# Denominator without the GpSimd pass, four chunk pairs to a logarithm visit, two diagonal convolutions, a new order

## The chip, the cores and the metric

One NeuronCore of a Trainium2 chip. Its engines run their own instruction streams in order and wait for each other by semaphores: TensorE (PE in the views, PEld for its weight loads), VectorE (DVE), ScalarE (ACT), GpSimd (POOL), and SyncE (SP), which here only issues DMAs. The metric is the device time of one execution in microseconds (us), lower is better.

## The reference

A causal convolution over time with softmax weights per head, then two feed-forward layers for 8192 tokens of 192 channels.

```python
w = softmax(weight, axis=-1)                       # 8 heads, 7 taps
x = sum_k w[head, k] * x_padded[:, s + k, :]       # (2, 4096, 192)
x = x.reshape(8192, 192)
gate = 1 / (1 + exp(-(x @ w_gate)))                # 192 -> 1536
x = (gate * (x @ w_val)) @ w_out                   # 1536 -> 192
h = x @ w_in                                       # 192 -> 2048
P = a[0] + a[1]*h + a[2]*h**2 + a[3]*h**3
Q = 1 + abs(b[0])*abs(h) + abs(b[1])*h**2
out = (P / (Q + 1e-6)) @ w_out2                    # 2048 -> 192
```

The matrices of both layers come as float64, two 32-bit words each, and the kernel turns them into float32 on the chip; x and the result are float32.

## The kernel before

The tokens stand along the free axis, in 16 tiles of 512. Each tile goes through three stages. `conv` makes the convolution of channels 0 to 127 (`ca`) and of 128 to 191 (`cb`, for two tiles at once). `moe1` is the gated layer in 12 chunks of 128 hidden channels, and `moe2` the rational layer in 16 chunks, which are taken in 8 pairs of 1024 columns. To keep float32 precision each matrix operand is split into a high part rounded to fp32r and the rest (`xha` and `xla`, `xhb` and `xlb`, `yha` and so on), so that a chunk of a 192-row product takes five matmuls (`mm192`, L656 to L660), and a chunk of an output product also five (L663 to L669). A tile takes 24 x 5 + 12 x 5 + 16 x 5 + 16 x 5 = 340.

`moe1`: the gate's and the value's sums land in PSUM banks `w` (four). ScalarE takes the sigmoid, VectorE multiplies by the value (L704), and the product is split into `r` tiles. At the end the sums `accb` are taken out of PSUM (L725 and its neighbours) and split into the y tiles, which `moe2` reads.

`moe2`, for one pair: ScalarE reads h from PSUM twice, as u = a3*h + a2 (two pointer operands, tile `av`) and as |h| (no pointer). VectorE makes the rest of P (L773, L775). GpSimd makes n = b1*|h| + b0 (L778), VectorE n*max(|h|, 1e-9) (L783). The quotient goes by a logarithm and a sigmoid, 1/(1 + q) = sigmoid(-ln q): ScalarE takes Ln and then Sigmoid of the pair, VectorE multiplies (L796), and the result is split: the high part by ScalarE, VectorE or GpSimd (L376, L375, L372), the rest by VectorE (L387). Ln and Sigmoid stand in different tables of ScalarE, so a change between them puts in an ACT_TABLE_LOAD. A visit to the logarithm takes two pairs (`batch`), so that a tile of 8 pairs makes four visits. `f` tiles (12 of 128x1024) hold s, u, |h| and n; `r` tiles (7) the split products.

The first tile's convolution differs: for channels 0 to 127 PE multiplies by seven diagonal matrices, made by VectorE from an identity (`conv_first`), and for the others VectorE runs the seven taps (L572, L575). Later tiles are convolved by GpSimd (L580, L583).

The order of all engines' instructions is decided when the program is built, by `Plan.order`: a list scheduler with costs of its own in ns, which takes the operation with the lowest priority number that can start. `PRM` holds offsets to the priorities (`off`), how many tiles each use may hold (`caps`), and what it costs in priority to hand a copy to another engine (`alt`). One line of the clock model reads

```python
step = 0.4473 if self.cols.get(w - 1, 0.0) >= BUSY else 0.8386
```

Of the kernel before, what the change touches and what calls it, by code (L numbers as in the profile page):

```python
# [75 lines left out]
class Plan:  # L76
# [72 lines left out]
    def order(self, look, switch):  # L149
# [78 lines left out]
        "g.m": 12836, "g.l": -14036, "gv": -503688, "gv.f": 39931, "gv.s": 21424, "gv.m": -105715,
        "ha": 14068, "ha.f": -9127, "ha.m": -20059, "ha.l": -563873, "hi1": -461921, "hi1.f": 117595,
        "hi1.m": 30632, "hi1.l": 9352, "hi2": 617179, "hi2.s": 28015, "hi2.l": -67281, "ld": 85904,  # L230
        "ld.m": 66018, "ln": -94912, "ln.f": 56900, "ln.s": 26766, "ln.m": -50067, "lo1": -192199,
        "lo1.f": -196745, "lo1.m": -47345, "lo1.l": 151726, "lo2": -186968, "lo2.f": -41762, "lo2.m": -14603,
# [5 lines left out]
        "wA.m": -6466, "wA.l": -16824, "wB": -78045, "wB.f": 31019, "wB.s": 8326, "wB.m": 53803, "wB.l": 1311,
        "wC": -20347, "wC.s": 22921, "wC.m": 34154, "wC.l": 40145, "wD": -203, "wD.f": 5940, "wD.s": -20677,
        "wD.m": -48332, "wD.l": 27289, "xs": -1058521, "xs.f": 114386, "xs.s": 6043, "xs.m": -67359,  # L240
        "xs.l": -82500, "y": -644733, "y.f": 64816, "y.s": -60589, "y.m": -7966, "ye": 91, "ye.f": -70525,
        "ye.s": -105007, "ye.m": 10681, "ye.l": 132694, "late": 6944, "ld.f": -71783, "lo2.s": -107566,
# [640 lines left out]
```

## Time and profile before

| | |
|---|---|
| median of 3 runs | 1328.44 us (1327.5 to 1329.65) |
| profiled execution, own time | 1329.45 us |
| its span | 1327.7 us |
| PE busy | 1279.2 us |
| VectorE busy | 1208.6 us |
| ScalarE busy | 1182.8 us |
| GpSimd busy | 654.0 us |

The span is the time from the program's first to its last instruction in the profile; the execution's own time holds a little more around it. A busy time is a union of instructions' times. PE's matmuls overlap in the records, so PE's own is no measure of how near it is to its best.

### The profile page before, as it was taken

The numbers are of one execution on the slowest core, as the hardware profiler recorded it, in microseconds if no ns is written. First come the engines' busy times: TensorE is split into PE (matmuls) and PEld (weight loads), VectorE is DVE, ScalarE is ACT, GpSimd is POOL, SyncE is SP. The second block draws the span as 40 slices with busy tenths as digits, with TensorE's granted clock in tenths as the row PEclk, the third lists the DMA queues.
The fourth block names the chain that finished last, engine by engine and source line by source line (L and its number), as shares of the span: only waits on it lengthen the run. The fifth ranks groups of instructions, "written<-read, shape, count | busy, mean of one in ns | idle before, by whom it ended". The sixth has DMA issues, their size and how long they took to land.

```text
span 1327.7 us, 15365 instructions
## 1 busy us (share of the span) xinstructions
PE 1279.2 (96%) x5478; PEld 1020.7 (77%) x5478; DVE 1208.6 (91%) x1410; ACT 1182.8 (89%) x1556; POOL 654.0 (49%) x450
## 2 busy tenths in 40 slices
PE   8889999999999999999999999999999999999996
PEld 4677778778777777788788877878787787877775
DVE  7889999999899989999888989899989998989897
ACT  6988989889998998889889988988989989999996
POOL 4166627735275542865429572394725836212131
PEclk9989999999999999999999999999999999999999
DMA  6621000000000000000000000000000000000000
GB/s 173 198 61 32 8 1 13 16 13 9 0 13 17 13 8 1 12 17 13 9 9 5 16 21 1 12 1 17 20 1 13 8 13 1 0 13 13 1 6 19
DMA packets 14317, 27.09 MB, mean 20 GB/s; under 512 B 2080, under 2 KB 5792, under 8 KB 14240
## 3 DMA queue, kind: packets, MB, share of 16 engines
q1 hardware_dynamic: 14240, 26.11, 6.7%
q8 instruction: 43, 0.70, 0.2%
q14 instruction: 34, 0.28, 0.1%
HBM read 19.81 MB, written 6.29 MB: 20 GB/s over the span
## 4 chain that ended last, share of the span: by engine, by line
PE 42%; DVE 26%; ACT 23%; issue 6%; DMA 2%; POOL 1%; SPq 0%; ACTq 0%; DVEq 0%; POOLq 0%
ACT f L376 14%; DVE r L387 6%; PE w L656 5%; PE w L657 5%; PE w L658 5%; PE w L660 5%; PE w L659 5%; DVE f L773 5%; ACT L376 4%; DVE f L775 4%; DVE f L783 4%; DVE f L796 3%; ACT r L376 2%; PE accd L668 2%; PE accd L669 2%
## 5 line engine op out<-in xcount | busy, mean ns | idle before, releaser
L778 POOL TENSOR_SCALAR f<-f,bv 128x1024 f32<-128x1024 f32 x128 | 189.2, 1479 | 435.2 <-ACT f L376 371.5
L376 ACT ACTIVATE f<-w 128x512 f32<-128x512 f32 x448 | 260.6, 599 | 48.9 <-PE w L660 25.4
L387 DVE TENSOR_TENSOR r<-f,r 128x1024 fp32r<-128x1024 f32 x224 | 292.1, 1316 | 10.6 <-ACT r L376 7.1
L376 ACT ACTIVATE f<-f 128x1024 f32<-128x1024 f32 (+3 forms) x288 | 286.6, 1002 | 1.5 <-DVE r L387 0.3
L376 ACT ACTIVATE f<-w,av 128x512 f32<-128x512 f32 x256 | 196.9, 778 | 43.8 <-PE w L660 39.1
L376 ACT ACT_TABLE_LOAD x160 | 205.3, 1283 | 2.9 <-DVE f L783 0.2
L376 ACT ACTIVATE r<-f 128x1024 fp32r<-128x1024 f32 x180 | 189.7, 1062 | 19.5 <-DVE f L704 9.8
L773 DVE TENSOR_TENSOR f<-f,w 128x512 f32<-128x512 f32 x256 | 170.5, 679 | 33.8 <-ACT f L376 32.9
L775 DVE SCALAR_TENSOR_TENSOR f<-f,av,w 128x512 f32<-128x512 f32 x256 | 187.0, 740 | 6.4 <-ACT f L376 3.3
L796 DVE SCALAR_TENSOR_TENSOR f<-f,av,f 128x1024 f32<-128x1024 f32 x128 | 175.1, 1380 | 12.8 <-ACT f L376 12.7
L783 DVE SCALAR_TENSOR_TENSOR f<-f,f 128x1024 f32<-128x1024 f32 x128 | 173.2, 1355 | 0.8 <-POOL f L778 0.6
L704 DVE TENSOR_TENSOR f<-f,w 128x512 f32<-128x512 f32 x192 | 130.3, 679 | 34.4 <-ACT f L376 23.0
L583 POOL TENSOR_TENSOR ca<-ca,tmp 128x512 f32<-128x512 f32 x90 | 154.2, 1713 | 6.0
L580 POOL TENSOR_SCALAR tmp<-xa,cw 128x512 f32<-128x512 f32 x90 | 115.4, 1282 | 8.4 <-DMA xa<-in_xt 1.4
L656 PE MATMUL w<-yha,w_h 128*128 128x512 f32 x256 | 102.1, 399 | 4.9 <-DVE f L775 3.2
L663 PE MATMUL accd<-r,wo_s 128*128 128x512 f32 x256 | 100.9, 394 | 4.9 <-ACT r L376 2.6
L668 PE MATMUL accd<-r,wo_s 128*128 128x512 f32 x256 | 100.8, 394 | 4.4 <-DVE r L387 4.3
L665 PE MATMUL accd<-r,wo_s 128*128 128x512 f32 x256 | 100.2, 391 | 0.3 <-DVE f L820 0.2
L669 PE MATMUL accd<-r,wo_s 128*128 128x512 f32 x256 | 100.2, 391 | 0.0
L664 PE MATMUL accd<-r,wo_s 128*128 128x512 f32 x256 | 100.0, 391 | 0.0
L657 PE MATMUL w<-yha,w_l 128*128 128x512 f32 x256 | 99.8, 390 | 0.0
L659 PE MATMUL w<-yhb,w_b 128*128 128x512 f32 x256 | 99.8, 390 | 0.0
(104 smaller groups left out, 2859.8 us busy)
## 6 DMA issues: line engine op xcount, KB each, us to landing
f<-in_wo SPq DMA_DIRECT2D x14, 384.0 KB, 3.3
xa<-in_xt SPq DMA_DIRECT2D x16, 259.0 KB, 2.8
out_dram<-f SPq DMA_DIRECT2D x16, 256.0 KB, 2.0
xb<-in_xt SPq DMA_DIRECT2D x16, 129.5 KB, 2.7
f<-in_w SPq DMA_DIRECT2D x4, 512.0 KB, 4.2
out_dram<-f SPq DMA_DIRECT2D x16, 128.0 KB, 2.3
f<-in_wg SPq DMA_DIRECT2D x4, 256.0 KB, 4.2
f<-in_wv SPq DMA_DIRECT2D x4, 256.0 KB, 4.8
```

Source lines behind the costliest of these rows:

```text
L376: plan.op("ACT", (53 if psum else 95) + n * 0.832 + 93 * ptr, prio, lambda: nc.scalar.activation(out=out(), in_=in_(), func=func, **kw), r ...
L387: dve(prio, n, lambda: nc.vector.tensor_tensor(out=out(), in0=in0(), in1=f(in1()), op=ALU.subtract), rd, wr, lock=lock, alts=alts)
L583: plan.op("POOL", 322 + 2.105 * n, p, lambda d=d: nc.gpsimd.tensor_tensor(out=y(), in0=y(), in1=T(d)[0:np_, 0:n], op=ALU.add), rd=[d, acc] ...
L656: nc.tensor.matmul(o, lhsT=wh.tile[:, c], rhs=ha, start=True, stop=False)
L657: nc.tensor.matmul(o, lhsT=wl.tile[:, c], rhs=ha, start=False, stop=False)
L659: nc.tensor.matmul(o, lhsT=wb.tile[:, c], rhs=hb, start=False, stop=False)
L704: dve(at("gv", t, p), n, lambda sc=sc, val=val: nc.vector.tensor_tensor(out=sc(), in0=sc(), in1=val(), op=ALU.mult), [(pv, "v"), (s, i)], ...
L773: dve(at("v", t, p), sn, lambda q=q, cut=cut, h=h: nc.vector.tensor_tensor(out=cut(u[q]), in0=cut(u[q]), in1=h(), op=ALU.mult), [ps_, (u[q ...
L775: dve(at("w", t, p), sn, lambda q=q, cut=cut, h=h: nc.vector.scalar_tensor_tensor(out=cut(u[q]), in0=cut(u[q]), scalar=av.tile[:, 1:2], in ...
L778: plan.op("POOL", 328 + 0.832 * gn, at("n", t, p), lambda q=q: nc.gpsimd.tensor_scalar(C(n[q]), C(ha[q]), bv.tile[:, 1:2], bv.tile[:, 0:1] ...
L783: dve(at("y", t, p), gn, lambda q=q: nc.vector.scalar_tensor_tensor(out=C(n[q]), in0=C(ha[q]), scalar=1e-9, in1=C(n[q]), op0=ALU.max, op1= ...
L796: dve(at("g", t, p), gn, lambda k=k: nc.vector.scalar_tensor_tensor(out=C(u[k]), in0=C(u[k]), scalar=av.tile[:, 0:1], in1=C(n[k]), op0=ALU ...
```

## The change

It does four things. The GpSimd pass over |h| goes: ScalarE's Abs scales by b1 while it reads (a pointer into a new tile `kv`), VectorE's one instruction makes (|b1 h| + b0)*|b1 h|, and the logarithm divides by b1 and adds a tiny constant through its own scale and bias (two pointers into `kv`). No `n` tile is used. A visit to the logarithm takes four pairs (`batch=[4, 4]`; the last tile keeps its four visits of two). The first tile's second convolution, like the first, becomes seven products with diagonal matrices on PE, and ScalarE copies its sum from PSUM to `cb`. And the offsets, caps and hand-over costs are new numbers, so that all engines' orders are new; in the clock model a column costs 0.4427 instead of 0.4473.

```diff
-            step = 0.4473 if self.cols.get(w - 1, 0.0) >= BUSY else 0.8386
+            step = 0.4427 if self.cols.get(w - 1, 0.0) >= BUSY else 0.8386
...
-        "A": -640, "A.f": 5683, "A.s": 4966, "A.m": 12771, "A.l": 26485, "B": 15953, "B.f": 8482,
+        "A": -2963, "A.f": -9114, "A.s": 6869, "A.m": 8851, "A.l": 10628, "B": 16339, "B.s": 720310,
...
-    caps=dict(u=7, n=8, ha=10, s=6, h1=3, l1=2, h2=2, l2=2, raw=3, t=9, dg=5),
+    caps=dict(u=12, ha=20, s=29, h1=13, l1=5, h2=2, l2=27, raw=8, t=3, dg=9),
...
-    batch=[2, 2, 2, 2],
+    batch=[4, 4],
...
-        dve(START + 90001, 1, lambda: nc.vector.tensor_scalar(
-            bv.tile[:, 0:1], bv.tile[:, 0:1], 1e-9, 0.0, op0=ALU.max, op1=ALU.add), [bv], [bv])
+
+        def ks():
+            k = kv.tile
+            nc.vector.tensor_scalar(k[:, 0:1], bv.tile[:, 1:2], 1e-15, 0.0, op0=ALU.max, op1=ALU.add)
+            nc.vector.reciprocal(k[:, 1:2], k[:, 0:1])
+            nc.vector.tensor_scalar(k[:, 1:2], k[:, 1:2], 1.0 / ONE, 0.0, op0=ALU.mult, op1=ALU.add)
+            nc.vector.memset(k[:, 2:3], 1e-18)
+        plan.op("DVE", 650, START + 90001, ks, rd=[bv], wr=[kv])
...
-            conv_taps("cb", t, p0 + step * 7, step, xb, 1, cb, len(two) * R, n, eng)
+            if t:
+                conv_taps("cb", t, p0 + step * 7, step, xb, 1, cb, len(two) * R, n)
+            else:
+                dma(START + 1, 128 * 512, lambda: nc.sync.dma_start(out=T(eye)[:, 0:128], in_=ident), [eye])
+                ca = conv_first(n, xa, 0, eye)
+                cp = conv_first(n, xb, 1, eye)
+                act(START + 19, n, lambda: T(cb)[:, 0:n], lambda: T(cp)[:, 0:n], [cp], [cb], psum=True)
...
-                act(at("ha", t, p), sn, lambda q=q, cut=cut: cut(ha[q]), h, [ps_], [(ha[q], j)], psum=True,
-                    func=ACTF.Abs)
+                act(at("ha", t, p), sn, lambda q=q, cut=cut: cut(ha[q]), h, [ps_, kv], [(ha[q], j)], psum=True,
+                    func=ACTF.Abs, scale=kv.tile[:, 0:1])
...
-            plan.op("POOL", 328 + 0.832 * gn, at("n", t, p), lambda q=q: nc.gpsimd.tensor_scalar(
-                C(n[q]), C(ha[q]), bv.tile[:, 1:2], bv.tile[:, 0:1], op0=ALU.mult, op1=ALU.add),
-                rd=[ha[q], bv], wr=[n[q]], lock=True, alts=[("DVE", 190 + 0.522 * gn, lambda q=q: nc.vector.tensor_scalar(
-                    C(n[q]), C(ha[q]), bv.tile[:, 1:2], bv.tile[:, 0:1], op0=ALU.mult, op1=ALU.add),
-                    True, H["n"]["DVE"])])
+
             dve(at("y", t, p), gn, lambda q=q: nc.vector.scalar_tensor_tensor(
-                out=C(n[q]), in0=C(ha[q]), scalar=1e-9, in1=C(n[q]), op0=ALU.max, op1=ALU.mult),
-                [ha[q], n[q]], [n[q]])
+                out=C(ha[q]), in0=C(ha[q]), scalar=bv.tile[:, 0:1], in1=C(ha[q]), op0=ALU.add, op1=ALU.mult),
+                [ha[q], bv], [ha[q]], ptr=1)
...
-                act(at("ln", t, p + 0.1 * i), gn, lambda k=k: C(n[k]), lambda k=k: C(n[k]), [n[j] for j in qs], [n[k]],
-                    func=ACTF.Ln, table="ln", scale=1.0 / ONE)
+                act(at("ln", t, p + 0.1 * i), gn, lambda k=k: C(ha[k]), lambda k=k: C(ha[k]),
+                    [*(ha[j] for j in qs), kv], [ha[k]], func=ACTF.Ln, table="ln", scale=kv.tile[:, 1:2], bias=kv.tile[:, 2:3])
```

The first place is ScalarE in the middle of the program, one whole visit to the logarithm before (an f tile out of the same f tile at 128x1024 is a logarithm, or a sigmoid behind the second load; `w,av` is u, `w` alone at f is |h| or a moe1 sigmoid):

```order
L376 ACT_TABLE_LOAD
L376 ACTIVATE f_4190<-f_4190 128x1024
L376 ACTIVATE f_4252<-w_4227,av 128x512
L376 ACTIVATE f_4211<-f_4211 128x1024
L376 ACTIVATE f_4252<-w_4239,av 128x512
L376 ACTIVATE f_4271<-w_4227 128x512
L376 ACTIVATE f_4271<-w_4239 128x512
L376 ACT_TABLE_LOAD
L376 ACTIVATE f_4217<-w_4254 128x512
```

and a visit now (`kv` marks the logarithm at 128x1024 and |b1 h| at 128x512):

```order
L378 ACT_TABLE_LOAD
L378 ACTIVATE f_4064<-f_4064,kv 128x1024
L378 ACTIVATE r_4281<-f_4209 128x1024
L378 ACTIVATE f_4140<-f_4140,kv 128x1024
L378 ACTIVATE f_4292<-w_4272,av 128x512
L378 ACTIVATE f_4160<-f_4160,kv 128x1024
L378 ACTIVATE f_4309<-w_4272,kv 128x512
L378 ACTIVATE f_4203<-f_4203,kv 128x1024
L378 ACTIVATE f_4292<-w_4302,av 128x512
L378 ACTIVATE f_4309<-w_4302,kv 128x512
L378 ACT_TABLE_LOAD
L378 ACTIVATE f_4335<-w_4286 128x512
```

Four logarithms stand between two loads instead of two, with PSUM reads that need no table between them in both.

The second place is VectorE at the start, where the low parts of tile 0's convolved input (`xlb`, `xla`) are made among the splits of the weights (`wg`, `wv`; `f` to `f` rows put their words together), before:

```order
L470 SCALAR_TENSOR_TENSOR f_169<-f_169,f_136 128x256
L470 SCALAR_TENSOR_TENSOR f_179<-f_179,f_140 128x256
L387 TENSOR_TENSOR xlb_192<-cb_138,xhb_187 64x512 x2
L387 TENSOR_TENSOR wv_l<-f_169,wv_h 128x256
L387 TENSOR_TENSOR wg_l<-f_179,wg_h 128x256
L470 SCALAR_TENSOR_TENSOR f_183<-f_183,f_146 128x256
L387 TENSOR_TENSOR xla_211<-w_151,xha_203 128x512
```

and now:

```order
L479 SCALAR_TENSOR_TENSOR f_239<-f_239,f_191 128x512
L479 SCALAR_TENSOR_TENSOR f_242<-f_242,f_203 128x512
L479 SCALAR_TENSOR_TENSOR f_247<-f_247,f_218 128x512
L389 TENSOR_TENSOR wv_l<-f_239,wv_h 128x512
L473 TENSOR_SCALAR f_237<-f_237 128x384
L389 TENSOR_TENSOR wg_l<-f_242,wg_h 128x512
L473 TENSOR_SCALAR f_245<-f_245 128x384
L389 TENSOR_TENSOR xlb_269<-cb_257,xhb_263 64x512 x2
L389 TENSOR_TENSOR wg_b<-f_247,wg_b 64x512
```

`xlb` was made between the first and the second column piece of the weights, and now stands among the fourth and last.

The third place is VectorE near the end, from the add that takes the last tile's moe1 sums out of PSUM (L725, now L733), before:

```order
L725 TENSOR_TENSOR f_10498<-f_10498,accb_10240 128x512
L387 TENSOR_TENSOR yla_10514<-accb_10239,yha_10507 128x512
L387 TENSOR_TENSOR r_10521<-f_10092,r_10509 128x1024
L387 TENSOR_TENSOR ylb_10530<-f_10498,yhb_10516 128x512
L387 TENSOR_TENSOR r_10534<-f_10175,r_10523 128x1024
L773 TENSOR_TENSOR f_10550<-f_10550,w_10536 128x512
L775 SCALAR_TENSOR_TENSOR f_10550<-f_10550,av,w_10536 128x512
```

and now:

```order
L733 TENSOR_TENSOR f_10244<-f_10244,accb_9822 128x512
L389 TENSOR_TENSOR r_10272<-f_9926,r_10262 128x1024
L389 TENSOR_TENSOR yla_10282<-accb_9821,yha_10270 128x512
L389 TENSOR_TENSOR ylb_10286<-f_10244,yhb_10276 128x512
L798 SCALAR_TENSOR_TENSOR f_9998<-f_9998,av,f_10030 128x1024
L798 SCALAR_TENSOR_TENSOR f_10074<-f_10074,av,f_10124 128x1024
L779 TENSOR_TENSOR f_10305<-f_10305,w_10291 128x512
```

Products of the tile before (L798, formerly L796) now stand behind the add: from here to the end there are 12 of them, where there were 8.

## Rows read from the trace of the kernel before

**Rows 1.** The page, busy time (share of the span) and instructions of each engine.

```profile
PE 1279.2 (96%) x5478; PEld 1020.7 (77%) x5478; DVE 1208.6 (91%) x1410; ACT 1182.8 (89%) x1556; POOL 654.0 (49%) x450
```

**Rows 2.** Timeline of PE: start, duration, line, tiles; first and last of fifteen.

```profile
23.64 0.39 PE L656 MATMUL w<-xha,wv_h 128*128 128x512 f32 x1
...
26.82 0.39 PE L660 MATMUL w<-xlb,wv_b 128*128 128x512 f32 x1
```

**Rows 3.** Table by stage: length; PE, PEld, DVE, ACT, POOL busy; clock, DMA share, GB/s.

```profile
0.00:154.70 154.70, 139.67 (x562) 105.07 (x563) 133.38 (x194) 129.43 (x217) 80.25 (x64) 0.97 0.34 100
154.70:1260.30 1105.60, 1085.07 (x4696) 873.85 (x4695) 1016.52 (x1151) 999.93 (x1273) 557.78 (x375) 1.00 0.03 10
1260.30:1327.70 67.40, 54.42 (x223) 41.80 (x222) 58.74 (x67) 53.46 (x68) 15.96 (x12) 0.97 0.04 12
0.00:20.00 20.00, 15.26 (x43) 6.66 (x44) 14.18 (x32) 12.02 (x30) 2.18 (x7) 0.98 0.68 188
40.00:60.00 20.00, 18.74 (x82) 14.88 (x81) 18.32 (x35) 17.57 (x33) 0.00 (x0) 1.00 0.80 229
```

**Rows 4.** Chain of work that ended last, 154.7 to 1260.3 us, shares by line.

```profile
by line: ACT f L376 15.1%; DVE r L387 5.9%; issue 5.5%; PE w L656 5.4%; ACT L376 5.0%; PE w L658 5.0%; PE w L660 4.9%; PE w L657 4.9%; PE w L659 4.9%; DVE f L773 4.4%; DVE f L775 3.9%; DVE f L783 3.4%; DVE f L796 3.3%; ACT r L376 2.7%; PE a
```

**Rows 5.** Waits, 154.7 to 1260.3 us: us in total, times, longest.

```profile
DVE f L773 <- ACT f L376: 28.2, 43, 1.8
DVE f L704 <- ACT f L376: 22.3, 24, 2.5
...
ACT f L376 <- DVE f L773: 9.8, 14, 1.6
ACT r L376 <- DVE f L704: 9.3, 10, 1.6
```

**Rows 6.** Groups, whole run: busy us, mean ns, idle before and its releasers.

```profile
L387 DVE TENSOR_TENSOR r<-f,r 128x1024 fp32r<-128x1024 f32 x224 | 292.1, 1316 | 10.6 <-ACT r L376 7.1 <-PE accb L665 1.6 <-PE accd L665 0.8
...
L376 ACT ACTIVATE f<-w 128x512 f32<-128x512 f32 x448 | 260.6, 599 | 48.9 <-PE w L660 25.4 <-DVE f L773 9.8 <-DVE f L775 6.2
L376 ACT ACT_TABLE_LOAD x160 | 205.3, 1283 | 2.9 <-DVE f L783 0.2
L376 ACT ACTIVATE f<-w,av 128x512 f32<-128x512 f32 x256 | 196.9, 778 | 43.8 <-PE w L660 39.1 <-DVE f L783 2.1 <-issue 1.8
L376 ACT ACTIVATE r<-f 128x1024 fp32r<-128x1024 f32 x180 | 189.7, 1062 | 19.5 <-DVE f L704 9.8 <-DVE f L796 7.2 <-PE accb L665 1.7
L778 POOL TENSOR_SCALAR f<-f,bv 128x1024 f32<-128x1024 f32 x128 | 189.2, 1479 | 435.2 <-ACT f L376 371.5 <-DVE r L387 31.1 <-DVE f L470 10.9
...
L796 DVE SCALAR_TENSOR_TENSOR f<-f,av,f 128x1024 f32<-128x1024 f32 x128 | 175.1, 1380 | 12.8 <-ACT f L376 12.7
L783 DVE SCALAR_TENSOR_TENSOR f<-f,f 128x1024 f32<-128x1024 f32 x128 | 173.2, 1355 | 0.8 <-POOL f L778 0.6
...
L601 PE MATMUL w<-xa,f 128*128 128x512 f32 x14 | 6.2, 592 | 0.0
```

**Rows 7.** Timeline of ScalarE around a table load.

```profile
640.18 1.28 ACT L376 ACT_TABLE_LOAD   x1
641.48 1.07 ACT L376 ACTIVATE f<-f 128x1024 f32<-128x1024 f32 x1
```

**Rows 8.** Groups of VectorE, 40 to 60 us.

```profile
L387 DVE TENSOR_TENSOR r<-f,r 128x1024 fp32r<-128x1024 f32 x3 | 3.6, 1215 | 0.0
```

**Rows 9.** Timeline of GpSimd and VectorE near 702 us.

```profile
701.69 1.29 POOL L583 TENSOR_TENSOR cb<-cb,tmp 128x512 f32<-128x512 f32 x1
...
702.41 1.65 DVE L783 SCALAR_TENSOR_TENSOR f<-f,f 128x1024 f32<-128x1024 f32 x1
```

**Rows 10.** Groups of VectorE, 1261 us to the end.

```profile
L796 DVE SCALAR_TENSOR_TENSOR f<-f,av,f 128x1024 f32<-128x1024 f32 x8 | 9.9, 1272 | 0.0
```

**Rows 11.** Timelines of VectorE and PE at the start.

```profile
15.52 1.37 DVE L387 TENSOR_TENSOR xlb<-cb,xhb 64x512 fp32r<-64x512 f32 x2
...
19.70 0.63 PE L660 MATMUL w<-xlb,wg_b 128*128 128x512 f32 x1
```

More of the change, by code (lines that the diff above doesn't have):

```diff
@@ L228 @@
[L228 to L232, printed above, removed]
@@ L238 @@
[L238 to L242, printed above, removed]
@@ new lines @@
+        "wD.m": -48332, "wD.l": 27289, "xs": -1582034, "xs.f": -67531, "xs.s": -43087, "xs.m": -14,
+        "xs.l": 309347, "y": -723473, "y.f": -161177, "y.s": 129907, "y.m": -107220, "ye": 42939,
+        "ye.s": -561715, "ye.m": 344612, "ye.l": -197564, "late": 5619, "lo2.s": 122206, "w.s": 99,
+        "cb.f": 16056, "cv.m": 1418, "y.l": -441, "w.m": 209751, "hi2.f": 198659, "ln.l": -40206,
+        "ld.l": 35649, "r.m": 179975,
+    },
+    look=dict(PE=24, ACT=0, DVE=0, POOL=2517, SP=0),
@@ L401, in conv_gated_rational_kernel @@
     bv = fixed([128, 2], F32, "bv")
+    kv = fixed([128, 3], F32, "kv")
     def small():
-        dma(START, 8000, lambda: nc.sync.dma_start(out=cw.tile, in_=wt), [cw])
+        dma(START - 1, 8000, lambda: nc.sync.dma_start(out=cw.tile, in_=wt), [cw])
         w, ng = cw.tile, wneg.tile
@@ L569, in y @@
                 return T(acc)[0:np_, 0:n]
-            if eng == "DVE":
-                if k == 0:
-                    dve(p, n // 2, lambda xin=xin, sc=sc: nc.vector.tensor_scalar(
-                        y(), xin(), sc(), 0.0, op0=ALU.mult, op1=ALU.add), [x, cw], [acc], ptr=1)
-                else:
-                    dve(p, n, lambda xin=xin, sc=sc: nc.vector.scalar_tensor_tensor(
-                        out=y(), in0=xin(), scalar=sc(), in1=y(), op0=ALU.mult, op1=ALU.add),
-                        [x, cw, acc], [acc], ptr=1)
-                continue
             d = acc if k == 0 else Buf("tmp")
@@ L585, in conv_taps, with conv_first @@
                     rd=[d, acc], wr=[acc], lock=200.0)
-    def conv_first(n, x):
-        eye, d, o = Buf("f", "t"), Buf("f", "dg"), Buf("w")
-        dma(START, 128 * 512, lambda: nc.sync.dma_start(out=T(eye)[:, 0:128], in_=ident), [eye])
+    def conv_first(n, x, i, eye):
+        d, o = Buf("f", "dg"), Buf("w")
         def diag():
@@ L617, in conv, with early @@
         t0, n = tiles[t]
-        p0, step, eng, ahead = (base - P, 4000.0, "POOL", 30000.0) if t else (START, 1.0, "DVE", 0.0)
+        p0, step = base - P, 4000.0
+        def early(cls, x):
+            return at(cls, t, x) if t else START + 1
         xa, ca = Buf("xa"), Buf("ca")
-        dma(at("ld", t, p0 - ahead), 512 * (n + HALO), lambda: nc.sync.dma_start(
+        dma(early("ld", p0 - 30000.0), 512 * (n + HALO), lambda: nc.sync.dma_start(
             out=T(xa)[:, 0:n + HALO], in_=tile_src(t, 0, 128)), [xa])
         if t:
-            conv_taps("cv", t, p0, step, xa, 0, ca, 128, n, eng)
+            conv_taps("cv", t, p0, step, xa, 0, ca, 128, n)
         else:
-            ca = conv_first(n, xa)
+            eye = Buf("f", "t")
         two, cb = conv_b.get(t, (None, None))
@@ L634, in ldb @@
                                       in_=tile_src(i, 128, D))
-            dma(at("ld", t, p0 + 1 - ahead), 256 * len(two) * (n + HALO), ldb, [xb], k=len(two))
-            conv_taps("cb", t, p0 + step * 7, step, xb, 1, cb, len(two) * R, n, eng)
+            dma(early("ld", p0 + 1 - 30000.0), 256 * len(two) * (n + HALO) * (1 if t else 2), ldb, [xb], k=len(two))
+            if t:
[5 more added lines that the diff above has]
+                act(START + 19, n, lambda: T(cb)[:, 0:n], lambda: T(cp)[:, 0:n], [cp], [cb], psum=True)
             conv_b.update({i: (two, cb) for i in two})
@@ L745, in moe2 @@
         last = t == NT - 1
-        sizes = K["tail"] if last else K["batch"] if nq == 8 else [2] * (nq // 2)
+        sizes = K["tail"] if last else K["batch"]
         ends = {sum(sizes[:i]) for i in range(len(sizes) + 1)}
```

63 lines of the change are left out of this document (32 added, 31 removed), and 4 rows, old and new, of the table off.

## The prediction

> **What bounds the kernel now.** The page comes first. Its busy line [rows 1] has TensorE at 96% of the span, VectorE at 91%, ScalarE at 89%, GpSimd at 49%. A busy PE is not a PE at its peak, so the next view is the timeline of PE in a stretch without waits: fifteen matmuls that start at 23.64 to 26.82 us [rows 2], 14 steps in 3.18 us, 0.227 us each. The 16 tiles need 16 x 340 = 5440 matmuls, 5440 x 0.227 = 1235 us. The span of 1327.7 us is 93 us above that, and this is what an order can win or lose.
>
> The table by stage [rows 3] says where these 93 us lie. I cut where tile 1's and tile 15's moe1 sums are taken out of PSUM (the add on L725, at 154.7 and 1260.3 us). The middle holds 4696 matmuls, 1066 us of work in 1105.6: 39.6 us of stalls. Behind 1260.3 us stand 223, 50.6 us in 67.4: 16.8 us lost. Ahead of 154.7 us stand 562, of which 38 are warm-up and the first convolution; 524 x 0.227 = 119 us, 35.7 lost. (An instruction across a cut is counted on both sides, which is under 1 us.)
>
> In the middle no engine is full (VectorE 1016.5 us of 1105.6, ScalarE 999.9), so the stalls are hand-over times. The chain of work that ended last, in this stretch [rows 4], shows what they are made of: table loads 5.0% (55 us; they are the ScalarE entry without a tile), other ScalarE work on f and r tiles 15.1 + 2.7% (197 us), the rest matmuls and VectorE. The waits [rows 5] say the same from the other side: VectorE waits 28.2 us for ScalarE before L773 and 22.3 us before L704. ScalarE waits for VectorE only 9.8 and 9.3 us. So ScalarE is the late one, VectorE is late behind it, and PE behind both.
>
> **The change, part by part.** Durations are the means of [rows 6].
>
> *Table loads.* In the whole program 160 before, 82 now. In the middle stretch the order has 148 before and 71 now: 77 x 1.283 = 98.8 us of ScalarE.
>
> What does a load cost beyond its 1283 ns? The timeline shows the next instruction 0.02 us behind a load's end [rows 7]; nothing else is to be had there. (The Trainium skill, "ScalarE: Activation LUTs", section "What ACT_TABLE_LOAD costs", puts 2.66 us on every switch, the load and a drain of about 1.38 us behind it. By that, 77 would give 205 us. This trace doesn't show the drain, and the sum stays at 1.283 us.)
>
> *Pointer operands.* The Abs gets a scale pointer, the logarithm a scale and a bias pointer. The trace has the PSUM read with two pointers (778 ns) and with none (599 ns): 179 ns for two. One pointer lies between 0 and 179; I take the half, 90 ns. In the middle 225 x 0.090 + 116 x 0.179 = 41.0 us of ScalarE come back. Copies to fp32r on ScalarE go from 154 to 142 there, 12 x 1.06 = 12.7 us less. Net for ScalarE: -98.8 + 41.0 - 12.7 = -70 us of 999.9, from 90% of the stretch to 84%.
>
> *The GpSimd pass.* L778 goes, 189.2 us of GpSimd. Most of the time GpSimd waited for its input (371.5 us, [rows 6]), not others for it. What its going can give is contention: a wide VectorE subtraction takes 1316 ns in the mean [rows 6] and 1215 ns in a stretch where GpSimd stands idle [rows 3, 8], and 480 wide VectorE instructions x 0.1 us are some 48 us in all. By GpSimd's busy time L778 has 189/654 of it, 14 us, the upper bound; the lower is none, as the timeline has VectorE stretched to 1.65 us beside L583 [rows 9], which stays. I take 3 us, nearer to that row. The 20 more fp32r casts on GpSimd (31 to 51) cost VectorE about as much: the two cancel. VectorE's product on L783 gets a pointer; L796, the same width with a pointer, is 25 ns longer in the mean: 128 x 0.025 = 3.2 us in the whole run. I take nothing for it, covered by VectorE's 89 us of idle time in the middle; without that cover it is 3 us.
>
> *What the middle gains.* Only what stands on the chain counts. Loads there are 55 us, of which 77/148 go: -29. The pointers lengthen the other ScalarE work (999.9 - 148 x 1.283 = 810 us) by 41.0, 5%, and it has 197 us of the chain: +10. Sum -19. The pass itself is not among the lines that [rows 4] names, all of 2.7% or more; I give it another -1. That makes **-20 us**. Bounds: 0, if another hand-over steps in each time, and -40, when no stall is left.
>
> *The end.* VectorE decides it: 58.7 us busy in the last 67.4 [rows 3]. It takes its instructions in order, so what stands behind the add that empties tile 15's moe1 sums has to be done before the end. Before, 8 L796 products stand there; now 12, as tile 14's second visit comes later: 4 x 1.272 = 5.1 us [rows 10]. All other wide kinds keep their count (13 subtractions, 8 of L783, 16 and 16 of half the width). GpSimd's casts behind the last convolution go from 9 to 22, up to 13 x 0.1 = 1.3 us of contention if each meets one wide instruction. I take **+6 us**, bounds +3 (some of it fits into pauses) and +11 (the casts cost what 1.65 against 1.215 us shows, 0.43 each).
>
> *The start.* The first sums of tile 0 need xlb. Before, VectorE made it as its 24th row, at 15.5 us, and the last of the first five matmuls started at 19.70 us [rows 11]. Now it stands behind the split of all four column pieces of both weights: 4.7 MB, with 0.5 MB of x ahead of them, at 188 to 229 GB/s [rows 3] 23 to 28 us. So the first whole group comes 5 to 10 us later. The two convolutions in a row on PE (6.2 us for seven products, [rows 6]) fit ahead of that and cost nothing; if the weights came at once, the second would cost its 6.2. Against this: all weights of moe1 are then there, so that PE's later waits for pieces of them have no cause, and only 468 matmuls instead of 541 stand ahead of tile 1's last sum; the 73 between, 16.6 us, move into the middle at full rate. ScalarE sets this stage (129.4 us busy of 154.7, [rows 3]); 13 rounding steps of weights move from it to VectorE and the sigmoids of the moved matmuls come later, but it starts late as well. I take **0**, bounds -10 and +12.
>
> Sum: -20 + 6 + 0 = -14 us. The profiled execution took 1329.45 us with its span of 1327.7, so 1.75 us lie around the span and are not touched; 1329.45 - 14 = 1315.4. The median of the runs is 1.0 us lower, hence **1314.5 us**.
>
> **The rivals.** *More than the chain says.* Once ScalarE has 70 us of air, VectorE's waits for it (28.2, 22.3, [rows 5]) go too, PE's stalls fall from 39.6 to some 8, and the end stays: -32 + 6 gives 1302.5 us. For it: those waits are larger than PE's stalls. Against: VectorE stays at 92% and must still hand over. (A switch worth 2.66 us, the rule of "ScalarE: Activation LUTs" in the Trainium skill, would end here as well, since the middle can't lose more than its stalls; no row bears it out, and I give it 0.02 of this rival's chance.)
>
> *Slower: buffers.* Four pairs to a visit hold u and ha of four pairs, 8 of the 12 f buffers, until logarithm, sigmoid, product and subtraction are done. Before, two pairs held six. If ScalarE then has to wait for VectorE to free a buffer, PE's four PSUM banks stay full. ScalarE's waits for VectorE are 9.8 and 9.3 us now [rows 5]; if they triple (+38) and half of that falls in front of PE, the gain is gone: -20 + 19 + 6 = +5 us; at full weight -20 + 38 + 6 = +24. I put it between, at 1340 us. It decides from 14 us of new stalls on. For it: 12 buffers as before. Against: one buffer fewer per pair (no n).
>
> *No change: the start.* xlb behind the last weight piece at the upper bound, 12 us not given back: -20 + 6 + 12 = -2, 1326.5 us. For it: the rates of [rows 3] give no more. Against: ScalarE's own work there shrinks.
>
> **How the numbers follow.** The forecast (1308 to 1321 us) gets 0.47, more gain 0.23, the start 0.13, the buffers 0.17. A measurement can tell about 0.2% (2.7 us) from no change: faster is below 1325.8 us, that is forecast, more gain and a good third of the start case, 0.75; same 0.08; slower 0.17. The range reaches from 1294 us (middle at -35, start at -5, end at +5) to 1334 us (buffers begun), leaving out some 0.08 below and 0.11 above.
>
> **What would show it.** 82 loads of 1283 ns; the logarithm near 1235 ns, the Abs near 690 ns. VectorE's waits for ScalarE before the successors of L773 and L704 down by a third or more, PE's stalls in the middle near 20 us. The stretch behind tile 15's add near 73 us, with VectorE saturated. The first matmul that reads xlb at 25 to 30 us. I am wrong if ScalarE's waits for VectorE grow by more than 14 us, or if tile 1's sums are taken out much later than 154.7 - 16.6 = 138 us.

## Result and profile after

The changed kernel takes 1335.55 us (median of 4 runs, 1334.83 to 1336.58), the kernel before in the same comparison 1327.97 us (4 runs, 1326.96 to 1329.65). The ratio is 1.0056, with a 95% interval of 1.0039 to 1.0074: slower by some 0.6%, where 1.1% faster was forecast. The profiled execution took 1335.36 us with a span of 1333.6 us, 5.9 us more than before.

The page's busy line of the changed kernel, to be held against [rows 1]:

```profile
PE 1284.8 (96%) x5492; PEld 1022.9 (77%) x5492; DVE 1203.8 (90%) x1418; ACT 1106.7 (83%) x1448; POOL 507.4 (38%) x342
```

ScalarE lost 76 us of busy time and GpSimd 147, VectorE 5, and the kernel became longer. The table by stage, cut at the same two adds (now L733, at 138.4 and 1262.2 us), answers to the first three of [rows 3]:

```profile
0.00:138.40 138.40, 125.01 (x493) 91.69 (x494) 119.00 (x191) 110.10 (x185) 69.60 (x55) 0.98 0.39 111
138.40:1262.20 1123.80, 1102.84 (x4772) 888.59 (x4771) 1022.41 (x1157) 935.81 (x1193) 425.80 (x279) 1.00 0.03 10
1262.20:1333.60 71.40, 56.95 (x230) 42.57 (x228) 62.37 (x70) 60.82 (x71) 11.97 (x9) 0.98 0.04 12
```

The stretches don't hold the same work, so I take 0.227 us off for each matmul, as the prediction did. Middle: 1123.8 - 4772 x 0.227 = 40.6 us of stalls, against 39.6 before. End: 71.4 - 230 x 0.227 = 19.2 us lost, against 16.8. Start: of 493, 52 are warm-up and the two convolutions (24 + 14 + 14 records), so 138.4 - 441 x 0.227 = 38.3, against 35.7. That is +1.0, +2.4 and +2.6 us, together the 6 us of the spans. The middle was to give 20 us and gave none. TensorE's granted clock is not the difference: it is 0.97, 1.00 and 0.97 in the three stretches before and 0.98, 1.00 and 0.98 now.

The groups of ScalarE in the middle show that the prices of the single instructions were right (the logarithm 1237 ns, the Abs 688, the loads 71 x 1283):

```profile
L378 ACT ACTIVATE f<-w,kv 128x512 f32<-128x512 f32 x230 | 153.3, 688 | 41.1 <-DVE f L781 13.4 <-DVE r L389 13.0 <-DVE f L779 7.4
L378 ACT ACTIVATE f<-f,kv 128x1024 f32<-128x1024 f32 x115 | 141.8, 1237 | 0.5
...
L378 ACT ACT_TABLE_LOAD x71 | 91.1, 1283 | 1.6 <-DVE r L389 0.2
```

ScalarE has 64 us less to do there (999.9 to 935.8). The waits of the middle say where they went:

```profile
ACT f L378 <- PE w L668: 71.9, 69, 4.4
DVE f L779 <- ACT f L378: 47.2, 50, 3.7
ACT f L378 <- DVE r L389: 38.1, 28, 5.3
ACT r L378 <- DVE f L712: 19.3, 13, 3.6
...
ACT f L378 <- DVE f L798: 14.4, 15, 2.1
ACT f L378 <- DVE f L781: 13.4, 20, 1.5
...
DVE f L712 <- ACT f L378: 11.9, 13, 2.7
```

Summed over all rows of this view, ScalarE waits 94.2 us for VectorE (34.1 before) and 81.7 us for PE (61.3 before), while VectorE's waits for ScalarE went up, from 73.1 to 85.8, instead of down by a third. ScalarE's waits for VectorE thus grew by 60 us; by the prediction's own sign of being wrong, 14 were enough. The 28.2 and 22.3 us of [rows 5] became 47.2 and 11.9. ScalarE's time was saved and then spent waiting. The chain of the same stretch confirms that the loads did leave it (3.3%, 5.0% in [rows 4]):

```profile
by line: ACT f L378 16.1%; PE w L664 6.4%; PE w L665 5.7%; PE w L668 5.7%; PE w L666 5.7%; PE w L667 5.7%; issue 5.6%; DVE r L389 4.9%; DVE f L798 4.0%; DVE f L781 3.4%; ACT L378 3.3%; DVE f L785 3.2%; DVE f L779 3.0%; ACT r L378 2.4%; PE a
```

### The profile page after: what moved, and what is told of

Its sections match the earlier page's. It is cut to its first block, busy times and chain, and to the rows that moved or that the text cites. A ratio compares the mean times of both kernels' runs of the same rounds, so it can differ in the third digit from the quotient of the medians.

```text
span 1333.6 us, 15135 instructions
## 1 busy us (share of the span) xinstructions
PE 1284.8 (96%) x5492; PEld 1022.9 (77%) x5492; DVE 1203.8 (90%) x1418; ACT 1106.7 (83%) x1448; POOL 507.4 (38%) x342
## 4 chain that ended last, share of the span: by engine, by line
PE 42%; ACT 25%; DVE 23%; issue 6%; DMA 2%; SPq 0%; DVEq 0%; ACTq 0%
ACT f L378 17%; PE w L664 6%; PE w L668 5%; PE w L665 5%; PE w L667 5%; PE w L666 5%; DVE r L389 5%; DVE f L798 4%; DVE f L781 3%; ACT L378 3%; DVE f L785 3%; DVE f L779 3%; ACT r L378 3%; DVE f L712 2%; PE accd L676 2%
## 5 line engine op out<-in xcount | busy, mean ns | idle before, releaser
L389 DVE TENSOR_TENSOR r<-f,r 128x1024 fp32r<-128x1024 f32 x224 | 291.2, 1307 | 16.8 <-PE accb L673 7.9
L374 POOL TENSOR_SCALAR r<-f 128x1024 fp32r<-128x1024 f32 x51 | 70.0, 1375 | 590.2 <-DVE f L798 208.5
L378 ACT ACTIVATE f<-w,kv 128x512 f32<-128x512 f32 x256 | 170.0, 688 | 44.7 <-DVE f L781 16.7
L378 ACT ACTIVATE r<-f 128x1024 fp32r<-128x1024 f32 x162 | 170.6, 1059 | 32.7 <-DVE f L712 22.5
L785 DVE SCALAR_TENSOR_TENSOR f<-f,bv 128x1024 f32<-128x1024 f32 x128 | 175.0, 1368 | 8.1 <-ACT f L378 7.9
L798 DVE SCALAR_TENSOR_TENSOR f<-f,av,f 128x1024 f32<-128x1024 f32 x128 | 176.1, 1388 | 5.1 <-ACT f L378 4.7
L583 POOL TENSOR_TENSOR ca<-ca,tmp 128x512 f32<-128x512 f32 x90 | 166.1, 1845 | 7.1
L378 ACT ACTIVATE f<-f,kv 128x1024 f32<-128x1024 f32 x128 | 157.8, 1237 | 0.6
L378 ACT ACTIVATE f<-f 128x1024 f32<-128x1024 f32 (+3 forms) x160 | 150.6, 960 | 4.4 <-DVE wo_s L531 2.1
L378 ACT ACTIVATE f<-w 128x512 f32<-128x512 f32 x192 | 113.6, 596 | 46.5 <-DVE r L389 21.4
L378 ACT ACT_TABLE_LOAD x82 | 105.2, 1283 | 1.8 <-DVE r L389 0.2
L676 PE MATMUL accd<-r,wo_s 128*128 128x512 f32 x256 | 100.3, 392 | 4.7 <-DVE r L389 4.7
L671 PE MATMUL accd<-r,wo_s 128*128 128x512 f32 x256 | 100.7, 393 | 3.5 <-POOL r L374 2.4
L673 PE MATMUL accd<-r,wo_s 128*128 128x512 f32 x256 | 100.2, 391 | 0.2 <-DVE f L822 0.2
L668 PE MATMUL w<-ylb,w_b 128*128 128x512 f32 x256 | 99.9, 390 | 0.3 <-DVE ylb L389 0.3
L672 PE MATMUL accd<-r,wo_s 128*128 128x512 f32 x256 | 100.1, 391 | 0.0
```

The source lines that it names most:

```text
L378: plan.op("ACT", (53 if psum else 95) + n * 0.832 + 93 * ptr, prio, lambda: nc.scalar.activation(out=out(), in_=in_(), func=func, **kw), r ...
L389: dve(prio, n, lambda: nc.vector.tensor_tensor(out=out(), in0=in0(), in1=f(in1()), op=ALU.subtract), rd, wr, lock=lock, alts=alts)
L583: plan.op("POOL", 322 + 2.105 * n, p, lambda d=d: nc.gpsimd.tensor_tensor(out=y(), in0=y(), in1=T(d)[0:np_, 0:n], op=ALU.add), rd=[d, acc] ...
L668: nc.tensor.matmul(o, lhsT=wb.tile[:, c], rhs=lb, start=False, stop=True)
L676: nc.tensor.matmul(a1, lhsT=w[:, 0, :], rhs=l, start=False, stop=last)
L785: dve(at("y", t, p), gn, lambda q=q: nc.vector.scalar_tensor_tensor(out=C(ha[q]), in0=C(ha[q]), scalar=bv.tile[:, 0:1], in1=C(ha[q]), op0= ...
```

## Experiments

Every kernel below keeps the order of instructions of the kernel that its name begins with, except where the edit says so: the plan is made first and only what an operation emits is changed. A number is the median, the ratio is to the kernel before in the same comparison. "Stall" is that of the middle stretch, worked out as above, cut at each kernel's own two adds. (For the kernel before the medians of these comparisons lay between 1327.4 and 1329.3 us; the ratio is taken between runs that stand beside each other and can differ from that of the medians by 0.2%, so a difference between rows of different comparisons is good to 2 or 3 us. Stall and busy times are those of the one profiled execution, which lies within 3.1 us of the median: 3.0 below it for before_abs_ptr, 2.8 below for before_f15 and after_sqrt, 2.1 above for after_ratio.)

```
kernel               us       ratio [95%]              stall   ScalarE, VectorE busy in the middle
before             1327.97    1                         39.6    999.9  1016.5
before_no_pass     1330.75    1.0011 [0.9999, 1.0024]   38.8    999.8  1013.8
before_abs_ptr     1342.23    1.0086 [1.0069, 1.0103]   47.0   1019.7  1014.7
before_new_arith   1352.11    1.0191 [1.0162, 1.0219]   57.3   1038.0  1017.5
before_no_loads    1313.57    0.9880 [0.9866, 0.9895]   24.6    808.7  1021.3
before_f15         1326.88    0.9988 [0.9976, 1.0000]   36.6    999.1  1015.8
after              1335.55    1.0056 [1.0039, 1.0074]   40.6    935.8  1022.4
after_imm          1321.54    0.9945 [0.9925, 0.9964]   27.9    896.9  1018.9
after_no_loads     1322.6     0.9951 [0.9934, 0.9967]   26.3    845.1  1019.3
after_imm_no_loads 1315.49    0.9909 [0.9892, 0.9925]   20.9    806.3  1015.4
after_dve_half     1322.33    0.9945 [0.9930, 0.9960]   30.1    934.6   966.5
after_imm_dve_half 1305.52    0.9833 [0.9819, 0.9848]   16.8    897.3   963.8
after_f15          1328.03    0.9994 [0.9985, 1.0004]   36.5    934.6  1021.5
after_pairs        1444.82    1.0862 [1.0846, 1.0878]  143.5   1044.1  1020.4
after_ratio        1326.22    0.9973 [0.9962, 0.9984]   29.9    907.0  1019.0
after_sqrt         1327.32    0.9978 [0.9968, 0.9988]   26.7    897.4  1016.5
```

The first theory was the prediction's rival *Slower: buffers*: visits of four hold the f tiles, so ScalarE waits for VectorE to free them. Its rival was that the stalls are VectorE's own.

### More f tiles

```diff
-    wo_s = weight([128, M1, 3, 128], "wo_s")
-    wo2_s = weight([128, M2, 3, 128], "wo2_s")
+    wo_s = weight([128, M1, 2, 128], "wo_s")
+    wo2_s = weight([128, M2, 2, 128], "wo2_s")
...
+    last = [-1] * 15
...
+                v.slot = min(range(15), key=lambda k: last[k])
```

> The changed kernel, same order on every engine, with 15 f tiles in place of 12 (each new use takes the f tile that came free first). To make room the low part of the output weights is written to a spare tile and its matmul reads the high part again, so the result leaves that part out; counts and shapes of the instructions stay. Theory A (buffers): ScalarE's added waits for VectorE are waits for an f tile, four-pair visits hold too many; expected 1315 to 1325 us, and ScalarE's waits for VectorE in the middle fall from 94 us to under 50. Theory B (VectorE sets the pace): a free tile earlier doesn't help, since VectorE is as late as before with everything; expected 1333 to 1337 us, and the waits move to another releaser.

> The kernel before in its own order with 15 f tiles in place of 12 (the third block of the split output weights is left out, as in the run of the changed kernel with 15). If it is the visit of four pairs that makes the changed kernel short of f tiles, the kernel before gains little: 1325 to 1329 us. If any order here is short of them, it gains as the changed kernel did, 7 us: 1319 to 1322 us.

The changed kernel came down by 7.5 us, to a place between the two theories' ranges; the kernel before by 2.0, as the first of its two ranges had it. In the middle the profiles differ less, by 4.1 and 3.0 us of stalls; in the changed kernel's the rest lies in the start (135.6 us instead of 138.4). With 15 tiles the 38.1 us of ScalarE's waits for the subtraction on L389 are gone, and ScalarE waits for PE instead (96.3 us, 71.9 above; the edit shifts the lines by one):

```profile
ACT f L378 <- PE w L669: 96.3, 85, 4.6
DVE f L780 <- ACT f L378: 45.2, 48, 3.7
ACT r L378 <- DVE f L713: 22.7, 15, 3.6
```

So the waits for f tiles were real. But over all rows ScalarE's waits for VectorE only fell from 94.2 to 59.6 us, not under 50, and of the 35 us that went, 4 came out as stalls. By the stalls the theory explains a small part, and not the difference between the two kernels' middles. By the medians it explains more: with 15 tiles in both, their ratios are 0.9994 and 0.9988, with intervals that overlap, so that most of the 0.6% that the change lost is gone. The profile of before_f15 lies 2.8 us under its median, and the start moves from run to run; whether the shortage of tiles costs the changed kernel some 1 us more than the kernel before or some 5 stays open.

### Loads and VectorE's product, each alone

```diff
-                    ..., func=ACTF.Ln, table="ln", ...)
+                    ..., func=ACTF.Identity, table="ln", ...)
```

```diff
-                out=C(ha[q]), in0=C(ha[q]), scalar=bv.tile[:, 0:1], in1=C(ha[q]), ...
+                out=C(ha[q])[:, 0:512], in0=C(ha[q])[:, 0:512], scalar=bv.tile[:, 0:1], in1=C(ha[q])[:, 0:512], ...
```

> The changed kernel, same order, with Identity in place of the logarithm, so that no table is loaded after the first (82 x 1.283 = 105 us of ScalarE gone; the quotient is left out of the result). Theory of the prediction (what stands on the chain counts): loads are 3.3% of the chain in the middle, 37 us, and 5 us in the end; expected 1295 to 1305 us. Theory B (VectorE sets the pace): ScalarE only waits longer; expected 1328 to 1336 us.

> The kernel before, same order, with Identity in place of the logarithm, so that no table is loaded after the first (160 x 1.283 = 205 us of ScalarE gone; the quotient is left out of the result). Theory of the prediction: loads are 55 us of the chain in the middle, where only 40 us of stalls can go; expected 1285 to 1300 us. Theory B: ScalarE was never what decided; expected 1320 to 1328 us.

> The changed kernel, same order, with VectorE's product on L785 cut to 512 of its 1024 columns (128 x 0.53 = 68 us of VectorE gone; the denominator of half of the columns is left out). Theory B (VectorE sets the pace): expected 1300 to 1315 us, most of the middle's 41 us of stalls and 4 us at the end. Theory A (buffers held by the visit): the tiles are held until the visit is done whatever this product takes; expected 1325 to 1334 us. Theory of the prediction (ScalarE late): 1330 us or more.

All three times lie between the ranges of the theories. All loads out of the kernel before, 160 x 1.283 = 205 us of ScalarE, gave 15 us. By the chain's share they stood for 55 us in the middle alone [rows 4]. This is the first place where the prediction's method fails: what stands on the chain is not what its removal gives. In the changed kernel 105 us of loads gave 13 us, and 61 us of VectorE (1203.8 to 1142.6 us busy, not the 68 that were expected) gave the same.

### The arithmetic, at the order of before

The pass alone, then the operand of the Abs, then those of the logarithm:

```diff
-            plan.op("POOL", ..., lambda q=q: nc.gpsimd.tensor_scalar(C(n[q]), C(ha[q]), bv.tile[:, 1:2], ...
+            plan.op("POOL", ..., lambda: None, ...
-                out=C(n[q]), in0=C(ha[q]), scalar=1e-9, in1=C(n[q]), op0=ALU.max, op1=ALU.mult),
+                out=C(n[q]), in0=C(ha[q]), scalar=bv.tile[:, 0:1], in1=C(ha[q]), op0=ALU.add, op1=ALU.mult),
```

```diff
-                    func=ACTF.Abs)
+                    func=ACTF.Abs, scale=kv.tile[:, 0:1])
```

```diff
-                    func=ACTF.Ln, scale=1.0 / ONE)
+                    func=ACTF.Ln, scale=kv.tile[:, 1:2], bias=kv.tile[:, 2:3])
```

> The kernel before in its own order, with the 128 GpSimd passes of the second mixture left out and nothing else moved: the product is (|h| + b0) |h|, so the scale of the logarithm's argument is left out (scale and bias stay immediate numbers). Ring theory (every engine waits for the next, and any link that goes gives back 7 to 20% of its busy time): the pass was a link between the Abs and the product, 128 x 0.75 us = 96 us of GpSimd, so 1316 to 1324 us. Rival (the pass lay beside other work): 1326 to 1330 us, as before.

> The kernel before in its own order, GpSimd pass left out, with the operand from memory on the Abs alone (256 x 0.09 = 23 us of ScalarE); the logarithm's scale stays an immediate number, so the scale of its argument is left out. Without any such operand this order took 1330.8 us, with all three 1352.1 us. Theory by place (the Abs is the last but one reader ahead of the products that give a PSUM bank back to TensorE, the logarithm is not): 1345 to 1352 us. Theory by amount (half of the operands' time, half of the loss): 1339 to 1343 us. If it is the logarithm's operands: 1331 to 1336 us.

> The kernel before in its own order and with visits of two pairs, but with the whole arithmetic of the change: no GpSimd pass, Abs with a scale from memory, the product with a number from memory, logarithm with scale and bias from memory. Against the run without the pass it adds only the operands from memory, some 46 us of ScalarE over the run. If the arithmetic is not what made the changed kernel slower: 1318 to 1327 us. If the operands from memory are: 1333 us or more.

The pass was hidden: without it GpSimd has 176 us less in the middle (1.48 us a pass [rows 6], not the 0.75 of the expectation), VectorE 2.7, and the time is the same within its interval. The operands cost 21 us, 11.5 for the Abs and 9.9 for the logarithm by the medians, 0.75 and 1.05% by the ratios: within what these can tell it goes by the amount, not by the place in the ring. In the middle, 38.2 us more of ScalarE made 18.5 us more of stalls. Four rows of the waits show a part of the way there, first without the operands (the table's second kernel):

```profile
DVE f L712 <- ACT f L376: 26.3, 26, 2.4
DVE f L779 <- ACT f L777: 20.5, 31, 1.8
PEld w L664 <- DVE f L781: 18.0, 36, 1.6
...
PEld accb L676 <- DVE r L387: 11.7, 17, 1.9
```

and with all of them:

```profile
DVE f L712 <- ACT f L376: 29.4, 29, 2.6
DVE f L779 <- ACT f L777: 28.2, 42, 2.0
PEld w L664 <- DVE f L781: 23.9, 43, 1.7
...
PEld accb L676 <- DVE r L387: 12.9, 18, 2.1
```

VectorE waits longer for ScalarE (over all rows 77.2 us became 95.6), and PE longer for the VectorE product that gives a PSUM bank back.

### The operands, at the changed order

```diff
-                    func=ACTF.Abs, scale=kv.tile[:, 0:1])
+                    func=ACTF.Abs)
...
-                    func=ACTF.Ln, scale=kv.tile[:, 1:2], bias=kv.tile[:, 2:3])
+                    func=ACTF.Ln, scale=1.0 / ONE)
```

> The changed kernel in its own order, with immediate numbers in place of the operands from memory of Abs and logarithm (the scale of the argument is left out), some 46 us of ScalarE less. By the 13 us that 105 us of ScalarE gave back in this order: 1329 to 1332 us. If the operands stretch the chain one for one: under 1310 us. If they are hidden: 1334 to 1337 us.

14 us came back, in none of the three ranges and more than the 4 to 7 us that the loads' rate (13 us for 105) had let me expect, and 38.9 us of ScalarE in the middle were worth 12.7 us of stalls. Without the operands the change would have been faster than before by 0.55%.

So there are four kernels, with and without the operands at either order. By the ratios the operands cost 1.8% at the order of before (1.0011 to 1.0191) and 1.1% at the changed one (0.9945 to 1.0056); the visits of four with the new order and the second diagonal convolution gain 0.7% without the operands and 1.35% with them. The sizes of the parts depend on which is changed first, their signs do not.

### The visit of four undone

```diff
+    for a in visits:
+        v = sorted(o.start for o in a)
+        for o, k in zip(a, (0, 1, 4, 5, 2, 3, 6, 7)):
+            o.start = v[k]
```

> The changed kernel with the order of one thing changed: in each visit of four pairs the eight places of ScalarE hold two logarithms, two sigmoids, two logarithms, two sigmoids, so that the loads come back (some 80 more, 1.28 us each, 100 us of ScalarE) and everything else stays where it is. By what loads gave back in the run without them (13 us for 105 us): 1345 to 1349 us, so the visit of four is a gain of 10 to 13 us. If the loads lie beside ScalarE's waits for VectorE, which the visit of four brings: 1335 to 1340 us.

Neither theory: 109 us for 82 more loads (164 in all, 82 x 1.283 = 105 us). A stretch of ScalarE's timeline shows how they fall:

```profile
720.44 1.28 ACT L378 ACT_TABLE_LOAD   x1
721.73 1.25 ACT L378 ACTIVATE f<-f,kv 128x1024 f32<-128x1024 f32 x1
723.00 1.28 ACT L378 ACT_TABLE_LOAD   x1
724.29 0.60 ACT L378 ACTIVATE f<-w 128x512 f32<-128x512 f32 x1
724.91 1.28 ACT L378 ACT_TABLE_LOAD   x1
726.20 1.24 ACT L378 ACTIVATE f<-f,kv 128x1024 f32<-128x1024 f32 x1
727.47 1.28 ACT L378 ACT_TABLE_LOAD   x1
728.76 0.60 ACT L378 ACTIVATE f<-w 128x512 f32<-128x512 f32 x1
```

The visit's places are not side by side: sigmoids of the first mixture (f<-w), which use the other table, stand between the second two logarithms. And where ScalarE is late here, PE stands still at once. The waits of the middle have, where the changed kernel had 15.4 and 4.6 us:

```profile
PEld w L665 <- ACT f L378: 89.6, 65, 3.7
...
PE w L665 <- ACT f L378: 62.8, 49, 3.3
```

Not all of the 109 us need be the loads'. TensorE's granted clock is 0.98 in this middle, where every other kernel of the table has 1.00. From 816 to 824 us PE is busy for 4.1 of 8 us; behind that, at a granted clock of 0.50 (the lower of its two levels, 1.2 GHz), its matmuls start 0.42 us apart instead of 0.23 (a row of a table by stage, then of PE's timeline):

```profile
824.00:826.00 2.00, 1.86 (x5) 0.95 (x4) 1.43 (x2) 1.06 (x3) 1.92 (x2) 0.50 0.00 0
```

```profile
826.31 0.63 PE L672 MATMUL accb<-r,wo_s 128*128 128x512 f32 x1
826.73 0.63 PE L673 MATMUL accb<-r,wo_s 128*128 128x512 f32 x1
```

By the mean of 0.98 the clock has at most some 25 of the 1227 us, an estimate from that rounded mean.

This is a price at the changed order, which was planned with visits of four. It doesn't say what these visits gained against the order of before.

### Two reliefs at once

> The changed kernel in its own order with both edits of ScalarE at once: immediate numbers in place of the operands from memory, and a plain scaled copy in place of the logarithm, so no table loads (scale of the argument and quotient left out); 46 + 105 us of ScalarE less. Alone they gave 14 and 13 us. If ScalarE sets the end only as far as the next bound: 1318 to 1322 us, as either alone. If their gains add: 1306 to 1310 us.

> The changed kernel in its own order with immediate numbers in place of the operands from memory, and the product (|h| + b0) |h| made on 512 of 1024 columns, 68 us of VectorE less (scale and half of the products left out). Alone the edits gave 14 and 13 us. If the bound left behind ScalarE is VectorE's: 1306 to 1312 us, the gains add. If it is neither's (TensorE's own work and the hand-overs): 1317 to 1322 us.

Both edits of ScalarE together gave 20 us, between the two ranges, the 14 of one and the 27 of the sum; in the middle 12.7 and 14.3 us of stalls alone, 19.7 together. ScalarE's edit and VectorE's gave 30 us, and in the middle 12.7 and 10.5 alone, 23.8 together: those add. So what is left after ScalarE is eased is largely VectorE, which the change had not eased at all in the middle (1016.5 us busy before, 1022.4 after):

```profile
135.40:1236.10 1100.70, 1093.31 (x4775) 892.16 (x4775) 963.77 (x1158) 897.28 (x1193) 401.71 (x279) 1.00 0.03 10
```

### Versions that keep the whole computation

With b0/b1 in the product, the Abs needs no operand and the logarithm only its scale:

```diff
-                    func=ACTF.Abs, scale=kv.tile[:, 0:1])
+                    func=ACTF.Abs)
...
-                out=C(ha[q]), in0=C(ha[q]), scalar=bv.tile[:, 0:1], in1=C(ha[q]), ...
+                out=C(ha[q]), in0=C(ha[q]), scalar=kv.tile[:, 1:2], in1=C(ha[q]), ...
...
-                    ..., scale=kv.tile[:, 1:2], bias=kv.tile[:, 2:3])
+                    ..., scale=kv.tile[:, 0:1])
```

With the weights scaled by the square root of b1 as they are split, neither needs one:

```diff
+        kw = dict(func=ACTF.Identity, scale=kv.tile[r, 0:1]) if cls == "wC" else dict(func=ACTF.Copy)
...
+            dve(prio, n, lambda: nc.vector.scalar_tensor_tensor(
+                out=out(), in0=in0(), scalar=kv.tile[r, 0:1], in1=f(in1()), op0=ALU.mult, op1=ALU.subtract), rd, wr)
```

> The changed kernel in its own order, nothing left out, with one operand from memory per pair in place of four (two Abs, two on the logarithm): the product is (|h| + b0/b1) |h| and the logarithm's scale b1, so the Abs takes no operand and the logarithm one, without the bias of 1e-18. 128 x 0.09 = 12 us of ScalarE are left of 46. With none of them this order took 1321.5 us. By the amount: 1324 to 1327 us. If place decides, and the logarithm's operand stands off the path: 1321 to 1323 us.

> The changed kernel in its own order, nothing left out, with no operand from memory on Abs or logarithm: the first weights of the second mixture are multiplied by the square root of b1 as they are split (in the copy and the difference that are there already), the polynomial's numbers and b0 are divided to fit, 14 instructions on single columns more at the start. As with immediate numbers: 1320 to 1324 us, faster than the kernel before by 0.3 to 0.6%. If the scale on the weights' copies delays the start: 1325 to 1330 us.

1326.22 us, by the amount as expected, and 1327.32 us, the expectation's case of a later start. Both are faster than the changed kernel, by 9 and 8 us, and than the kernel before by 0.27% (0.16 to 0.38) and 0.22% (0.12 to 0.32). Their middles are nearly as short as without operands (29.9 and 26.7 us of stalls, 27.9 with immediate numbers). What they lack in their profiles against the run with immediate numbers lies mostly at the start: tile 1's add stands at 141.7 and 141.1 us, there at 136.8. Over the profiles of the changed order it lies anywhere from 135.4 to 143.1 us; what moves it wasn't settled, and so whether the scaled weight copies cost something there stays open too.

## Why the prediction was wrong

**What failed** is the step "What the middle gains". It forecast -20 us, from -29 for the loads, +10 for the operands and -1 for the pass; measured is +1.0. The runs split it by stalls: without the pass 39.6 became 38.8 (-0.8); with the operands 38.8 became 57.3 (+18.5, not +10); the visits of four with the new order made 40.6 of that (-16.7, not -29). Taken the other way round, the visits and the order made 27.9 of 38.8 (-10.9), and the operands 40.6 of that (+12.7): either way the gain is smaller and the cost larger than forecast. Both large terms took an engine's share of the chain as the rate at which time on it is lost or won. The share is neither. For the operands, 24% of ScalarE's other work was on the chain, and 48% of the added time became stalls. For the loads, 29% was on the chain (55 of 148 x 1.283 = 190 us), and all of them out of the kernel before gave 15.0 us of stalls, 8%.

There is no one rate. At a fixed order it grows with what ScalarE has to do in the middle: at the order of before 8% of the time between 809 and 1000 us of it became stalls (the loads), 41% from there to 1020 (the Abs) and 56% from there to 1038 (the logarithm); at the changed order 16% from 845 to 936 us (the loads), 33% from 897 to 936 (the operands) and 95% from 936 to 1044 (the loads put back, part of it the clock's). VectorE has 1014 to 1022 us in all of these. A reading of this is that ScalarE's time is cheap as long as VectorE, 91% busy, is the one that is waited for, and dear once ScalarE has as much to do. That is argued, not shown: each of these steps took or added something else at another place.

How much of the -16.7 is the visits' and how much the new order's isn't settled: no run here has one without the other. The sum had no term for waits for f tiles either; they are taken up under the rivals.

**Table loads** and **pointer operands**: 71 loads of 1283 ns in the middle and 82 in all, the Abs 688 and the logarithm 1237 ns, as forecast. ScalarE fell by 64 us, against 70; of the 12 copies that were to leave it in the middle, 9 did (155 to 146). (The 2.66 us a switch of the Trainium skill, "ScalarE: Activation LUTs", section "What ACT_TABLE_LOAD costs", again has no row here: the 82 loads undone cost 109 us, 1.33 each, not 218.)

**The GpSimd pass** was put at 3 us of VectorE and 1 us of the middle, rightly: 2.7 us of VectorE, 0.8 us of stalls, and the same time within the interval.

**The end**: +6 forecast for the stretch, +4.0 measured (67.4 to 71.4), within its bounds. "VectorE decides it" is not borne out in full: it is busy for 62.37 of the 71.4 us, 87% as before, and with 3.9 us less of it there (after_dve_half) the stretch is 1.1 us shorter. The twelve products are there, at the place that was named:

```profile
L798 DVE SCALAR_TENSOR_TENSOR f<-f,av,f 128x1024 f32<-128x1024 f32 x12 | 15.1, 1279 | 1.6 <-ACT f L378 1.6
```

**The start**: 0 forecast, +2.6 measured, within its bounds and within what it varies by. The first matmul on xlb starts at 28.95 us (25 to 30 was said; 19.70 in [rows 11]) after a wait of 6.49 us, and tile 1's add stands at 138.4 us where 138 was worked out. That agreement is in part luck: 83 matmuls fewer stand ahead of it in the traces (441 for 524), 18.8 us and not 16.6, and 2.6 us more are lost.

```profile
28.18 0.80 PE L667 MATMUL w<-xhb,wg_b 128*128 128x512 f32 x1 [6.49 <-ACT xhb L378]
28.95 0.79 PE L668 MATMUL w<-xlb,wg_b 128*128 128x512 f32 x1
```

**The rivals.** *Slower: buffers* gave 1340 us and the right side; ScalarE's waits for VectorE tripled nearly as it described, on the rows that it would have (L389, L798). 15 tiles took back 7.5 us of the changed kernel's time and 4 us of its stalls, 2.0 and 3 in the kernel before: the waits were mostly time that ScalarE had over, yet the shortage is a part of the loss, of some 1 to 5 us. The operands are the larger part, 14 us at the changed order. Either of the two taken away alone brings the kernel back to the time of before, within the interval, or under it (0.9994 and 0.9945). *More than the chain says* failed as its own argument against it said: VectorE stayed at 91% of the middle and was still waited for. *No change: the start* was wrong in its place.

In medians, then: +2 us without the pass (not to be told from none), +21 by the operands, and -17 by the visits of four and the new order together, their loss at the end included; by the ratios +0.1, +1.8 and -1.35%.

## What to carry to other kernels

On a ring of engines that wait for each other and are nearly all 85 to 95% busy, an engine's share of the chain doesn't price a change on it: here a microsecond of ScalarE was worth 0.08 to 0.33 us of stalls where ScalarE had under 1000 us in the middle, and 0.41 to 0.95 where it was pushed past that, and two reliefs added up when they fell on different engines, not when they fell on the same one. Cost small additions to every instruction (90 ns for an operand from memory, 512 times) at a third to half of their time, and look for an algebra that needs none before trading something for them. Two edits that are planned together are best run apart at a fixed order, with what each emits changed and the order kept: here one such run, the operands at the order of before, shows the loss (1.8%).

## What was not expected of the hardware

Taking 176 us of wide GpSimd work out of the middle shortened VectorE's busy time by only 2.7 us: its wide subtraction took 1321 ns beside the passes and 1327 without them. And a table load is 1283 ns wherever it stands, but 160 of them taken out of the kernel before gave 0.10 us each at the end (15 us), while 82 put into the changed one cost 1.33 us each (109 us, with a granted clock of 0.98 in the middle instead of 1.00).
